# The convolution branch of an adaLN block: two nested running sums per tile in place of three products

## The chip, the core and the metric

The kernel runs on one core of a Trainium2 chip. The core has five engines with queues of their own: TensorE (PE, matrix products, with its weight loads shown apart as PEld), VectorE (DVE), ScalarE (ACT), GpSimd (POOL) and SyncE (SP, which here only issues DMAs). Each engine works through its own instructions strictly in the order in which they were written and waits on semaphores for the others. Products land in PSUM, where the kernel holds three accumulators `dn`, the bank `CV` of the convolution branch and four banks that `bank()` hands out in turn; everything else lies in SBUF or in device memory.

The metric is the device time of one execution in microseconds (us). Lower is better.

## The reference

`x` is 2048 tokens of 448 channels in float32. With `mod = silu(c) @ w_mod` cut into six rows `sa, ca, ga, sb, cb, gb`, the reference computes

```
h = layernorm(x) * (1 + ca) + sa
x = x + ga * A(h)                     # a state space model as a long convolution
h = layernorm(x) * (1 + cb) + sb
x = x + gb * ((silu(h @ w_gate) * (h @ w_up)) @ w_down)     # w_gate, w_up: 448x1792, w_down: 1792x448
```

where `A(h)[t, d] = sum over s <= t of K[d, t-s] * h[s, d], plus h[t, d] * Dskip[d]`, and `K[d, l]` is the real part of a sum over 256 complex exponentials in `l`.

## The kernel before, in words

**The small path.** When the exponents are small enough (a flag, computed on the chip, decides it, and with these inputs it does), the kernel takes `K[d, l]` as a straight line in `l`: `k0[d] + k1[d] * l`. The convolution is then made of running sums over tokens. Multiplied by `ga`, the two coefficients are kept as rows that are spread over all 128 partitions, `gm0` and `gm1` (which shares its tile with `g0`), and the gated skip row is `gd`. A running sum within a tile of 128 tokens is one product with a 128x128 triangle of ones, `tri`. What the tiles before add up to is carried as a row, `run0` and `run1`, which is added to the tile's first row ahead of the product; after the product the last row is copied out (to partition 127 of `run`, by way of the slice `end`, partitions 96 to 127) and a small DMA brings it to partition 0.

**Tiles and blocks.** The 2048 tokens are 16 tiles of 128. The feed-forward part treats them in six blocks of 2, 2, 3, 3, 3 and 3 tiles (`TILES`). In each block `f` runs over 14 slices of 128 hidden channels. For each `f`, `gate_up(f)` makes 22 products on PE (line 758), each as wide as the block (256 or 384 columns); ACT takes the silu (773), DVE multiplies (788), ACT rounds the result to `phi` (795) and DVE keeps the rest as `plo` (796); `down(f-1)` adds three products per tile into `dn` (808). The two halves of a split number, high and low, are each in fp32r, a form of float32. In the chain of work of the profile one fp32r product of 448 columns is a step of 0.20 us, one in plain float32 a step of 0.75 us. In the first block (`fresh`) the weights are still being loaded by DMAs on SP, and ACT and DVE split them into high and low parts on the way (lines 122 and 125 for `w_gate` and `w_up`, 115 and 117 for `w_down`).

**What sets the order.** The order is written out by hand (`manual_schedule`). While block `b` runs through the feed-forward part, the convolution branch of the next block's tiles is woven in: a table, `TIMES`, gives for each tile the half-steps at which its stages are recorded. Half-step `2f` stands right behind `gate_up(f)`, half-step `2f+1` right behind `down(f-1)`. The row of `TIMES` is the first for block 0, the second for block 1 and the third for all later blocks. All that a stage puts on PE, DVE, ACT, POOL or SP goes into that engine's queue at that place. In the first block and before it, two tiles are treated in a long opening part, whose order is the string `PLAN`.

**The stages before the change** are the functions of `small_path`. `s0` makes `h`, `s1` makes `v0 = h*gm0` and `v1 = h*gm1`, where `gm0` has meanwhile been lowered by the token's place in its tile times `gm1` (line 732, `ntok`). `s2` adds the carried rows (962, 963) and splits `v0` into `vh` and `vl` (970, 971). `s4` makes three products: `tri` with `vh` and `vl` into the bank `CV`, and `tri` with `v1` into one of the four banks that `gate_up` uses too (982 to 984). `s5` copies the carried rows out (1003 to 1005) and adds both sums to `x`, the second one times the token's place in its tile, `tok` (1006, 1007). For block 0's two tiles the first product is taken in plain float32 (`s4f`, 994 and 995).

`CV` is one PSUM bank. What is written there next has to wait until everything that reads the earlier contents is done.

Of the kernel before, what the change touches and what calls it, by code (L numbers as in the profile page):

```python
# [8 lines left out]
F32 = mybir.dt.float32  # L9
# [34 lines left out]
m1 cpc k1 gd h11 hd0 ck v01 sq0 o10 v10 w0 cbw o12 v11 o01 o02 hd1 w01 o13 o14 fs xh1 gc0 sa d00 gc1 st0 r0 sp x1 st1 r1 l1 spc n10 gq fl n11 D0 qtb sbt sbc  # L44
# [12 lines left out]
def tile_kernel(ctx, tc, x, a_re, a_im, b_re, b_im, c_re, c_im, log_dt,  # L57
# [71 lines left out]
    tok = const.tile([128, 1], F32)  # L129
# [8 lines left out]
    gm1 = g0  # L138
    ones = const.tile([128, 1], F32)
    halves = const.tile([128, 2], F32)  # L140
    mhalf, half = halves[:, 0:1], halves[:, 1:2]
    ntok = const.tile([128, 1], F32)
# [144 lines left out]
    with tc.tile_pool(name="pre", bufs=1) as pre:  # L287
# [20 lines left out]
        po.iota(tok, pattern=[[1, 1]], base=0, channel_multiplier=1, allow_small_or_imprecise_dtypes=True)  # L308
        po.iota(ntok, pattern=[[1, 1]], base=0, channel_multiplier=-1, allow_small_or_imprecise_dtypes=True)
# [25 lines left out]
        for z in range(2):  # L335
# [20 lines left out]
        h01, v0, v1, hd, h2 = ([pre.tile([128, w], t, name=f"{n}_{q}") for q in range(2)] for n, t, w in  # L356
                               (("h", F32, D), ("v0", F32, D), ("v1", F32R, D), ("hd", F32, D), ("h2", F32, 512)))
# [114 lines left out]
        def flag_of():  # L472
# [43 lines left out]
            "fr1": copy(run1[end], CV[end, 0:D]), "fx": copy(xs[0], DN[0][:, 0:D]),  # L516
# [204 lines left out]
    def first_rows():  # L721

        ve.tensor_tensor(run0[end], run1[end], DN[1][end, 0:D], op=OP.add)
# [6 lines left out]
    def gate_0():  # L730

        ve.scalar_tensor_tensor(gm0, gm1, ntok, gm0, op0=OP.mult, op1=OP.add)

    def run_blocks(pools, stages, first=None):
# [150 lines left out]
        for b, ts in enumerate(TILES):  # L885
            todo = {}
            if b + 1 < len(TILES):
# [16 lines left out]
                if b == 0 and first is None:  # L904
                    go(EXTRA[0], gate_0)
                    todo["mid"] = [(first_rows, ())]
                    at(0, 1, lambda: sy.dma_start(run[0:1], run[127:128]))
# [33 lines left out]
    def small_path(pools):  # L941
# [10 lines left out]
        def s1(i, on_v=False):  # L952
            h = vs[i]
            v0 = v0_of(i)
            v1 = work.tile([128, D], F32R, name="v1", bufs=2)
            for v, g in ((v0, gm0), (v1, gm1)):
                (ve if on_v else po).tensor_tensor(v, h, g, op=OP.mult)  # L957
            vs[i] = h, v0, v1

        def rows(i):  # L960
            h, v0, v1 = vs[i]
            ve.tensor_tensor(v0[0:1], v0[0:1], run0[0:1], op=OP.add)
            ve.tensor_tensor(v1[0:1], f32(v1[0:1]), run1[0:1], op=OP.add)

        def s2(i):
            rows(i)
            h, v0, v1 = vs[i]
            vh = work.tile([128, D], F32R, name="vh")
            vl = work.tile([128, D], F32R, name="vl")
            sc.copy(vh, v0)  # L970
            ve.tensor_tensor(vl, v0, f32(vh), op=OP.subtract)  # L971
            vs[i] = h, vh, vl, v1

        def s3(i, on_v=False):
            h = vs[i][0]
            (ve if on_v else po).tensor_tensor(h, h, gd, op=OP.mult)  # L976

        def s4(i):
            h, vh, vl, v1 = vs[i]
            o = CV[:, 0:D]  # L980
            s = bank()[:, 0:D]
            pe.matmul(o, tri, vh, start=True, stop=False)  # L982
            pe.matmul(s, tri, v1, start=True, stop=True)  # L983
# [133 lines left out]
```

## Time and profile before

| | |
|---|---|
| median of three runs | 471.46 us (470.68 to 472.36) |
| the profiled execution | 470.78 us, of which 469.0 us is the span from its first to its last instruction |
| granted TensorE clock, mean | 0.997 |
| PE busy | 459.0 us (98%) |
| DVE busy | 282.1 us (60%) |
| ACT busy | 160.5 us (34%) |
| POOL busy | 63.4 us (14%) |
| opening part, until the first product of `gate_up` | 31.75 us |
| block 0 (from 31.7 us) | 56.8 us |
| block 1 (from 88.5 us) | 55.5 us |
| blocks 2, 3 and 4 | 80.5 us each |
| block 5 with the tail | 83.5 us |

The span is the time from the first instruction to the last; 1.8 us of the execution lie outside it. The busy time of an engine is the time in which it had an instruction under way. Matmuls are pipelined, so the duration of one is longer than the step from one to the next: 12 products of 448 columns have a duration of 365 ns each, but the chain of work goes from one to the next in 200 ns. The view that follows the chain of work back from the last instruction gives these steps, and is the better price list for PE. Spans on POOL are rough.

### The profile page before, as it was taken

Reading aid. Unit: us, or ns where it says so; the run is one execution under the profiler, and the core shown is the slowest. Engines: PE = TensorE matmul, PEld = TensorE weight load, DVE = VectorE, ACT = ScalarE, POOL = GpSimd, SP = SyncE. Lnnn points to the kernel's source line nnn. Section 1 sums busy time; section 2 is a strip of 40 time slices with the busy share of each in tenths; the row PEclk is TensorE's granted clock in tenths of the full one; section 3 lists DMA queues with packets and bytes.
Section 4 is the critical chain, followed back from the end, with each engine's and each line's share of the span. In section 5 each row is a group of like instructions: output and inputs, shape, how many; then the busy total and the mean of one; then the engine's idle time right before and its main releaser. Section 6 shows DMA issues by size and latency. Waiting matters only on the chain.

```text
span 469.0 us, 7027 instructions
## 1 busy us (share of the span) xinstructions
PE 459.0 (98%) x2735; PEld 438.0 (93%) x2735; DVE 282.1 (60%) x539; ACT 160.5 (34%) x363; POOL 63.4 (14%) x88
## 2 busy tenths in 40 slices
PE   6899999999999999999999999999999999999995
PEld 4579999999999999999999999999999999999995
DVE  4888999778866447573754766374566543222225
ACT  5888666522343122233212223311223222221111
POOL 1232001000000223200022410003141000000000
PEclk9999999999999999999999999999999999999998
DMA  8976652110003000111300011130001112000001
GB/s 309 405 251 189 211 178 91 58 42 2 2 0 100 0 1 0 46 46 46 117 2 0 2 45 46 45 119 1 1 16 31 46 45 80 22 1 1 1 0 64
DMA packets 18778, 31.24 MB, mean 67 GB/s; under 512 B 2608, under 2 KB 13488, under 8 KB 18736
## 3 DMA queue, kind: packets, MB, share of 16 engines
q1 hardware_dynamic: 18096, 30.53, 19.3%
q8 instruction: 23, 0.38, 0.4%
q10 hardware_dynamic: 640, 0.18, 0.2%
q14 instruction: 19, 0.16, 0.1%
HBM read 24.61 MB, written 6.03 MB: 65 GB/s over the span
## 4 chain that ended last, share of the span: by engine, by line
PE 95%; issue 2%; DMA 1%; POOL 0%; ACT 0%; DVE 0%; POOLq 0%; ACTq 0%
PE bank L758 61%; PE dn L808 28%; DMA vec<-in_c_log_dt_dram 1%; PE dn L480 1%; PE bank L983 1%; PE cv L982 1%; PE bank L836 1%; PE cv L984 1%; PE bank L227 0%; PE bank L266 0%; PE bank L403 0%; PE cv L995 0%; PE bank L437 0%; ACT L339 0%; PE cv L375 0%
## 5 line engine op out<-in xcount | busy, mean ns | idle before, releaser
L758 PE MATMUL bank<-hhi,gu 128*128 128x384 f32 (+1 forms) x1176 | 208.9, 317 | 0.1
L758 PEld LDWEIGHTS bank<-hhi,gu 128*128 128x128 f32 x1176 | 189.4, 188 | 3.0 <-issue 0.8
L758 PE MATMUL bank<-hlo,gu 128*128 128x384 f32 (+1 forms) x672 | 130.8, 317 | 0.0
L758 PEld LDWEIGHTS bank<-hlo,gu 128*128 128x128 f32 x672 | 109.1, 188 | 0.2
L788 DVE TENSOR_TENSOR bank<-raw,bank 128x384 f32<-128x384 f32 (+1 forms) x69 | 36.9, 534 | 117.9 <-PE bank L758 115.4
L795 ACT CAST phi<-bank 128x384 fp32r<-128x384 f32 (+1 forms) x83 | 36.7, 443 | 137.9 <-DVE bank L788 137.9
L773 ACT ACTIVATE raw<-bank 128x384 f32<-128x384 f32 (+1 forms) x70 | 32.8, 469 | 119.4 <-PE bank L758 103.7
L796 DVE TENSOR_TENSOR plo<-bank,phi 128x384 fp32r<-128x384 f32 (+1 forms) x83 | 42.5, 512 | 37.5 <-ACT phi L795 37.5
L808 PE MATMUL dn<-wdh,phi 128*128 128x448 f32 x218 | 57.6, 365 | 0.0
L808 PE MATMUL dn<-wdh,plo 128*128 128x448 f32 x218 | 57.2, 363 | 0.0
L808 PE MATMUL dn<-wdl,phi 128*128 128x448 f32 x218 | 56.9, 362 | 0.0
L808 PEld LDWEIGHTS dn<-wdh,plo 128*128 128x128 f32 x218 | 40.8, 187 | 3.0 <-DVE plo L796 0.3
L808 PEld LDWEIGHTS dn<-wdl,phi 128*128 128x128 f32 x218 | 40.9, 187 | 2.7
L808 PEld LDWEIGHTS dn<-wdh,phi 128*128 128x128 f32 x218 | 38.7, 188 | 1.6 <-ACT p L773 0.2
L185 POOL TENSOR_SCALAR rsb<-mvb 128x1 f32<-128x1 f32 (+2 forms) x13 | 4.4, 337 | 142.6 <-DVE mvb L157 142.6
L125 DVE TENSOR_TENSOR gu<-raw,gu 128x1024 fp32r<-128x1024 f32 x14 | 17.0, 1218 | 0.9 <-ACT gu L123 0.9
L185 POOL TENSOR_SCALAR rsa<-mva 128x3 f32<-128x3 f32 (+1 forms) x6 | 2.3, 380 | 98.4 <-DVE mva L157 96.1
L957 POOL TENSOR_TENSOR m<-m,gm 128x448 f32<-128x448 f32 x9 | 10.4, 1155 | 20.8 <-DVE m L202 17.1
L971 DVE TENSOR_TENSOR vl<-m,vh 128x448 fp32r<-128x448 f32 x12 | 9.1, 757 | 6.7 <-ACT vh L970 6.1
L122 ACT CAST gu<-raw 128x768 fp32r<-128x768 f32 x14 | 11.6, 832 | 0.0
L976 POOL TENSOR_TENSOR m<-m,gd 128x448 f32<-128x448 f32 x9 | 11.5, 1281 | 0.0
L215 ACT ACTIVATE raw<-raw,rsb 128x64 f32<-128x64 f32 x14 | 4.8, 345 | 18.9 <-DVE raw L212 9.7
(237 smaller groups left out, 411.7 us busy)
## 6 DMA issues: line engine op xcount, KB each, us to landing
raw<-in_B_w_gate_up_dram SPq DMA_DIRECT2D x14, 512.0 KB, 3.8
rawd<-in_B_w_down_dram SPq DMA_DIRECT2D x16, 224.0 KB, 3.9
x<-in_A_u_dram SPq DMA_DIRECT2D x12, 224.0 KB, 2.8
out_dram<-x SPq DMA_DIRECT2D x11, 224.0 KB, 1.9
xd<-raw SPq DMA_DIRECT2D x9, 256.0 KB, 2.0
raw<-xd SPq DMA_DIRECT2D x36, 64.0 KB, 1.9
wm<-in_w_mod_groups_dram SPq DMA_DIRECT2D x5, 448.0 KB, 8.2
wm<-in_w_mod_groups_dram SPq DMA_DIRECT2D x5, 336.0 KB, 8.2
```

The lines of the kernel that those rows point to most:

```text
L122: sc.copy(wgu[j][:, :, 0:3, :], w[:, :, 0:3, :])
L125: ve.tensor_tensor(wgu[j][:, :, 3:7, :], w[:, :, ::-1, :], f32(wgu[j][:, :, 0:4, :][:, :, ::-1, :]), op=OP.subtract)
L185: po.tensor_scalar(rs[:, 0:n], self.mv[:, 0:n, 1], EPS, None, op0=OP.add)
L758: pe.matmul(ps[s][:, 0:n], w[:, s, a], (hlo if lo else hhi)[:, k, first_col(n):first_col(n) + n], start=first and q == 0, stop=end and q = ...
L773: sc.activation(p[:, 0:n], ps[0][:, 0:n], AF.Silu)
L788: ve.tensor_tensor(ps[1][:, 0:n], p[:, 0:n], ps[1][:, 0:n], op=OP.mult)
L795: sc.copy(hi[:, 0:n], ps[1][:, 0:n])
L796: ve.tensor_tensor(lo[:, 0:n], ps[1][:, 0:n], f32(hi[:, 0:n]), op=OP.subtract)
L808: pe.matmul(dn[q][:, 0:D], u[:, cs], v, start=f == 0 and z == 0, stop=f == (NF - 3 if last else NF - 1) and z == 2)
L957: (ve if on_v else po).tensor_tensor(v, h, g, op=OP.mult)
L971: ve.tensor_tensor(vl, v0, f32(vh), op=OP.subtract)
L976: (ve if on_v else po).tensor_tensor(h, h, gd, op=OP.mult)
```

## The change

The branch is computed by two running sums, one inside the other. The first, `u`, is the running sum of `h` itself. The second, `v`, is the running sum of `w = u*gm1`; since a running sum of a running sum weighs each token by how far back it lies, `u*(gm0-gm1) + v` is what was made before from `v0`, `v1` and the token's place. `gma` holds `gm0-gm1`.

From the second block on, `h` is rounded to `hh` for the first product, and what the rounding left off is multiplied by `gm0` and added into `w`, so that the second product carries it. In block 0 the first product takes `h` in plain float32 and there is no rest. Per tile there are thus two products, `u` (`s4` or `s4f`) and `v` (`s6`), and both are written to `CV`.

The stages become eight: `s0` (`h`), `s1` (`h*gd`, on POOL), `s2` (carried row, rounding, rest), `s3` (the rest times `gm0`, and the skip added to `x`, both on POOL), `s4` (`u`), `s5` (`w`, the first carried row out, `u*gma` added to `x` by POOL), `s6` (`v`), `s7` (the second carried row out, `v` added to `x`). In block 0, `row` and `skip` stand in the places of `s2` and `s3`. Each carried row has a DMA of its own (`carry`), for block 0's tiles on SP, for the others on ACT.

The opening part makes `hh` for its two tiles and sums these in `left_over`; `gate_0`, run early in block 0, turns the opening part's last rows into the new carried rows by three POOL instructions, and the DMA of that row moves from `f = 0` to `f = 2`. `tok`, `ntok` and their two iotas go.

The core of the diff (of the table `TIMES` only the row of block 0 is shown; `...` marks what is left out):

```diff
 TIMES = (
-    ((1, 3), 5, ((5, 10, 13, 15, 15, 16), (9, 9, 17, 19, 20, 20)), 20, (22, 23)),
+    ((1, 3), 5, ((5, 6, 7, 8, 10, 10, 14, 14, 16), (8, 9, 12, 13, 15, 15, 18, 18, 20)), 20, (22, 23)),
...
         def left_over():
             for q in range(2):
-                pe.matmul(CV[:, 0:D], all1, v1[q], start=q == 0, stop=q == 1)
+                pe.matmul(CV[:, 0:D], all1, hh[q], start=q == 0, stop=q == 1)
...
-            "fr1": copy(run1[end], CV[end, 0:D]), "fx": copy(xs[0], DN[0][:, 0:D]),
+            **{f"hh{q}": copy(hh[q], h01[q]) for q in range(2)}, "fr1": copy(run0[end], CV[end, 0:D]), "fx": copy(xs[0], DN[0][:, 0:D]),
...
     def first_rows():
-        ve.tensor_tensor(run0[end], run1[end], DN[1][end, 0:D], op=OP.add)
+        ve.tensor_copy(run1[end], DN[1][end, 0:D])
...
     def gate_0():
-        ve.scalar_tensor_tensor(gm0, gm1, ntok, gm0, op0=OP.mult, op1=OP.add)
+        t = v0_of(2)[end]
+        po.tensor_tensor(gma, gm0, gm1, op=OP.subtract)
+        po.tensor_tensor(t, run0[end], gma[end], op=OP.mult)
+        po.tensor_tensor(run1[end], run1[end], t, op=OP.subtract)
...
-                    at(0, 1, lambda: sy.dma_start(run[0:1], run[127:128]))
+                    at(2, 1, lambda: sy.dma_start(run[0:1], run[127:128]))
...
-        def s1(i, on_v=False):
+        def s1(i):
+            po.tensor_tensor(v0_of(i), vs[i], gd, op=OP.mult)
+
+        def row(i):
             h = vs[i]
-            v0 = v0_of(i)
-            v1 = work.tile([128, D], F32R, name="v1", bufs=2)
-            for v, g in ((v0, gm0), (v1, gm1)):
-                (ve if on_v else po).tensor_tensor(v, h, g, op=OP.mult)
-            vs[i] = h, v0, v1
...
+            ve.tensor_tensor(h[0:1], h[0:1], run0[0:1], op=OP.add)
 
         def s2(i):
-            rows(i)
-            h, v0, v1 = vs[i]
-            vh = work.tile([128, D], F32R, name="vh")
-            vl = work.tile([128, D], F32R, name="vl")
-            sc.copy(vh, v0)
-            ve.tensor_tensor(vl, v0, f32(vh), op=OP.subtract)
-            vs[i] = h, vh, vl, v1
+            row(i)
+            h = vs[i]
+            hh = work.tile([128, D], F32R, name="hh")
+            sc.copy(hh, h)
+            ve.tensor_tensor(h, h, f32(hh), op=OP.subtract)
+            vs[i] = h, hh
+
+        def skip(i):
+            po.tensor_tensor(xs[i], xs[i], v0_of(i), op=OP.add)
+
+        def s3(i):
+            h = vs[i][0]
+            po.tensor_tensor(h, h, gm0, op=OP.mult)
+            skip(i)
+
+        def s4f(i):
+            u = CV[:, 0:D]
+            pe.matmul(u, f32(tri), vs[i], start=True, stop=True)
+            vs[i] = None, u
 
         def s4(i):
-            h, vh, vl, v1 = vs[i]
-            o = CV[:, 0:D]
-            s = bank()[:, 0:D]
-            pe.matmul(o, tri, vh, start=True, stop=False)
-            pe.matmul(s, tri, v1, start=True, stop=True)
-            pe.matmul(o, tri, vl, start=False, stop=True)
-            ve.tensor_tensor(xs[i], h, xs[i], op=OP.add)
-            vs[i] = o, s
...
+            h, hh = vs[i]
+            u = CV[:, 0:D]
+            pe.matmul(u, tri, hh, start=True, stop=True)
+            vs[i] = h, u
+
+        def carry(i, k, row):
+            if i + 1 < NT:
+                sc.copy(run[end, k, :], row[end])
+                (sy if i in TILES[1] else sc).dma_start(run[0:1, k, :], run[127:128, k, :])
 
         def s5(i):
-            o, s = vs.pop(i)
-            if i + 1 < NT:
-                sc.copy(run1[end], s[end])
-                ve.scalar_tensor_tensor(run0[end], run1[end], 128.0, o[end], op0=OP.mult, op1=OP.add)
-                (sy if i in TILES[1] else sc).dma_start(run[0:1], run[127:128])
-            ve.tensor_tensor(xs[i], xs[i], o, op=OP.add)
-            ve.scalar_tensor_tensor(xs[i], s, tok, xs[i], op0=OP.mult, op1=OP.add)
+            h, u = vs[i]
+            t = work.tile([128, D], F32, name="t")
+            w = work.tile([128, D], F32R, name="w")
+            ve.tensor_tensor(t if h is not None else w, u, gm1, op=OP.mult)
+            if h is not None:
+                ve.tensor_tensor(w, t, h, op=OP.add)
+            ve.tensor_tensor(w[0:1], f32(w[0:1]), run1[0:1], op=OP.add)
+            carry(i, 0, u)
+            ve.tensor_tensor(t, u, gma, op=OP.mult)
+            po.tensor_tensor(xs[i], xs[i], t, op=OP.add)
+            vs[i] = w
+
+        def s6(i):
+            v = CV[:, 0:D]
+            pe.matmul(v, tri, vs[i], start=True, stop=True)
+            vs[i] = v
+
+        def s7(i):
+            v = vs.pop(i)
+            carry(i, 1, v)
+            ve.tensor_tensor(xs[i], xs[i], v, op=OP.add)
+
+        return lambda b: (s0, s1, s2, s3, s4, s5, s6, s7) if b else (s0, s1, row, skip, s4f, s5, s6, s7)
```

How this moves instructions is seen best in block 0, around `f = 7`. In the rows below, `tri` is the triangle, `m` with a number is the tile that holds `h`, `w` the weighted first sum, `dn` the accumulators of `down`, `gu` the weights of `gate_up`, `wdl` the low part of a slice of `w_down`, and `x_74` and `x_75` are block 0's two branch tiles, the first and the second. On PE, before, the two products of the first tile stand behind `down(6)`, the plain float32 one last:

```order
L808 MATMUL dn_68<-wdh_664,plo 128x448
L808 MATMUL dn_69<-wdh_664,plo 128x448
L994 MATMUL bank<-v_766,tri 128x448
L995 MATMUL cv<-m_79,tri 128x448
L758 MATMUL bank<-hhi,gu_662 128x256 x7
```

On PE, now, the first tile's second sum (1007) stands ahead of `down(6)` and the second tile's first sum (978) behind it:

```order
L1007 MATMUL cv<-w,tri 128x448
L809 MATMUL dn_68<-wdh_667,phi 128x448
L809 MATMUL dn_69<-wdh_667,phi 128x448
L809 MATMUL dn_68<-wdl_668,phi 128x448
L809 MATMUL dn_69<-wdl_668,phi 128x448
L809 MATMUL dn_68<-wdh_667,plo 128x448
L809 MATMUL dn_69<-wdh_667,plo 128x448
L978 MATMUL cv<-m_79,tri 128x448
L759 MATMUL bank<-hhi,gu_665 128x256 x7
```

Two products that both write `cv` now have one `down`, six products, between them, and the second of them is of another tile. On DVE, before, at the same `f`:

```order
L788 TENSOR_TENSOR bank<-p,bank 128x256
L125 TENSOR_TENSOR gu_709<-raw,gu_709 128x2x512
L796 TENSOR_TENSOR plo<-bank,phi 128x256
L976 TENSOR_TENSOR m_79<-m_79,gd 128x448
L997 TENSOR_TENSOR x_74<-m_79,x_74 128x448
L1004 SCALAR_TENSOR_TENSOR run<-run,cv 32x448
L1006 TENSOR_TENSOR x_74<-x_74,cv 128x448
L1007 SCALAR_TENSOR_TENSOR x_74<-bank,tok,x_74 128x448
L117 TENSOR_TENSOR wdl_764<-rawd_83,wdh_763 128x448
```

And on DVE, now:

```order
L789 TENSOR_TENSOR bank<-p,bank 128x256
L126 TENSOR_TENSOR gu_714<-raw,gu_714 128x2x512
L797 TENSOR_TENSOR plo<-bank,phi 128x256
L1013 TENSOR_TENSOR x_74<-x_74,cv 128x448
L996 TENSOR_TENSOR w<-cv,g_89 128x448
L999 TENSOR_TENSOR w<-w,run 1x448
L1001 TENSOR_TENSOR t<-cv,gma 128x448
L118 TENSOR_TENSOR wdl_768<-rawd_83,wdh_767 128x448
```

The reader of the first tile's second sum (1013) stands behind the feed-forward's multiply, the split of a weight slice and `plo`; behind it come the readers of the second tile's first sum (996, 1001), with the carried row between them (999). On POOL, block 0 had only small instructions of the norms from the branch on:

```order
L1048 COMPARE_AND_BRANCH
L177 TENSOR_SCALAR cs<-mva 128x1
L178 TENSOR_SCALAR mva<-mva 128x1
L177 TENSOR_SCALAR cs<-mva 128x1
L178 TENSOR_SCALAR mva<-mva 128x1
L185 TENSOR_SCALAR rsa<-mva 128x2
L186 TENSOR_TENSOR rsa<-rsa,halves 128x2
L177 TENSOR_SCALAR cs<-mvb 128x1
```

Now the three instructions of `gate_0` stand ahead of the norms' small ones (they are lines 731, 732 and 733, of which the first, `gma<-gm_90,g_89`, has 128 partitions and the other two have 32), and the branch's work follows the norms:

```order
L185 TENSOR_SCALAR rsa<-mva 128x2
L186 TENSOR_TENSOR rsa<-rsa,halves 128x2
L954 TENSOR_TENSOR m_79<-m_79,gd 128x448
L969 TENSOR_TENSOR x_74<-x_74,m_79 128x448
L954 TENSOR_TENSOR m_79<-m_79,gd 128x448
L1002 TENSOR_TENSOR x_74<-x_74,t 128x448
L969 TENSOR_TENSOR x_75<-x_75,m_79 128x448
L1002 TENSOR_TENSOR x_75<-x_75,t 128x448
L177 TENSOR_SCALAR cs<-mvb 128x1
```

Nine instructions of 448 columns, the three of `gate_0` among them, have come to POOL in this block: for each tile the skip row (954), its addition to `x` (969) and the addition of the first sum's share (1002).

More of the change, by code (lines that the diff above doesn't have):

```diff
@@ L138, in tile_kernel @@
     gm1 = g0
+    gma = const.tile([128, D], F32)
     ones = const.tile([128, 1], F32)
@@ L141, in tile_kernel @@
     mhalf, half = halves[:, 0:1], halves[:, 1:2]
-    ntok = const.tile([128, 1], F32)
     pick = const.tile([128, 1], F32)
@@ L355, in tile_kernel @@
         sca = pre.tile([128, N], F32)
-        h01, v0, v1, hd, h2 = ([pre.tile([128, w], t, name=f"{n}_{q}") for q in range(2)] for n, t, w in
-                               (("h", F32, D), ("v0", F32, D), ("v1", F32R, D), ("hd", F32, D), ("h2", F32, 512)))
+        h01, v0, v1, hd, hh, h2 = ([pre.tile([128, w], t, name=f"{n}_{q}") for q in range(2)] for n, t, w in
+                               (("h", F32, D), ("v0", F32, D), ("v1", F32R, D), ("hd", F32, D), ("hh", F32R, D), ("h2", F32, 512)))
         qt = {n: pre.tile([128, 512], F32, name="qt" + n) for n in "gcs"}
```

26 lines of the change are left out of this document (4 added, 22 removed), and 2 rows, old and new, of the table TIMES.

## The prediction

> **What bounds the kernel now.** I read the engines' busy times first, then the shares of the chain of work, then the busy times by stage, and last the chain itself.
>
> ```profile
> PE 459.0 (98%) x2735; PEld 438.0 (93%) x2735; DVE 282.1 (60%) x539; ACT 160.5 (34%) x363; POOL 63.4 (14%) x88
> PE 95%; issue 2%; DMA 1%; POOL 0%; ACT 0%; DVE 0%; POOLq 0%; ACTq 0%
> core 0: us, PE busy (x) PEld busy (x) DVE busy (x) ACT busy (x) POOL busy (x), PEclk, DMA share, GB/s
> 31.70:88.50 56.80, 56.75 (x410) 54.11 (x411) 52.55 (x97) 40.77 (x95) 5.44 (x10) 1.00 0.48 147
> 144.00:224.50 80.50, 80.50 (x445) 78.75 (x444) 45.12 (x82) 21.53 (x44) 14.74 (x17) 1.00 0.11 35
> ```
>
> PE is the bound: 95% of the chain. But the stages differ. Over the whole span DVE is busy for 60%, in block 2 (144.0 to 224.5) for 56%, in block 0 (31.7 to 88.5) for 52.55 of 56.80, which is 93%. A product saved is a gain in either, as long as PE is not made to wait for DVE, and in block 0 DVE has 4.25 us to spare in all.
>
> **What each tile loses on PE.** The chain in block 2, around one tile's products, by start and step:
>
> ```profile
> 170.30 3.81 PE bank L758 x22
> 174.12 0.20 PE cv L982
> 174.32 0.21 PE bank L983
> 174.53 0.20 PE cv L984
> 174.73 1.80 PE dn L808 x9
> ```
>
> Three products take 0.61, so one is 0.203. The twelve tiles 4 to 15 each lose one (two remain, each of the same width): 12 x 0.203 = 2.44 us gained. The products now stand alone between `gate_up` and `down`, not three in a row; each of the rows above has the same 0.20 whether a product follows another form or its own, so I take 0.20 for a lone one. Block 0's two tiles are the ones made here for block 1:
>
> ```profile
> 58.10 2.51 PE bank L758 x22
> 60.61 1.20 PE dn L808 x6
> 61.81 0.20 PE bank L994
> 62.02 0.75 PE cv L995 x2
> 62.77 2.60 PE bank L758 x22
> ```
>
> They have 0.20 and 0.75 before, and still do: the plain product is now that of `h`, the other that of `w`. No gain here.
>
> **The bank `CV` in block 0.** Here the change adds a wait. Before, one of a tile's two products in block 0 was written there, and two `f` lay between the tiles (the chain above has the first tile's at 62.02). Now the first tile's second sum (1007) is written to `CV` behind `gate_up(7)`, and the second tile's first sum (978) behind `down(6)`, six products later. It must wait until DVE has read the former (1013), and behind that wait stands all of PE's work.
>
> When does PE get there? `gate_up(7)` ends at 60.61 in the row above; the first tile's plain product now stands ahead of it, so 61.36; the second sum 0.20, `down(6)` 1.20: 62.76.
>
> When is DVE done with 1013? DVE goes strictly in order, and in this stretch it is the row of instructions itself that counts:
>
> ```profile
> 47.18 0.42 DVE L788 TENSOR_TENSOR bank<-p,bank 128x256 f32<-128x256 f32 x1
> 48.98 0.61 DVE L117 TENSOR_TENSOR wdl<-rawd,wdh 128x448 fp32r<-128x448 f32 x1
> 49.60 0.43 DVE L788 TENSOR_TENSOR bank<-p,bank 128x256 f32<-128x256 f32 x1
> 51.41 0.68 DVE L200 SCALAR_TENSOR_TENSOR m<-x,mva,ca 128x448 f32<-128x448 f32 x1
> 52.84 0.62 DVE L957 TENSOR_TENSOR m<-m,gm 128x448 f32<-128x448 f32 x1
> 53.38 0.62 DVE L957 TENSOR_TENSOR v<-m,g 128x448 fp32r<-128x448 f32 x1
> 59.66 0.60 DVE L962 TENSOR_TENSOR m<-m,run 1x448 f32<-1x448 f32 x1
> 61.26 0.41 DVE L788 TENSOR_TENSOR bank<-p,bank 128x256 f32<-128x256 f32 x1
> 63.06 0.60 DVE L976 TENSOR_TENSOR m<-m,gd 128x448 f32<-128x448 f32 x1
> ```
>
> From one multiply (788) to the next, with nothing of the branch between, are 2.42 us (47.18 to 49.60). `h` for a tile (200, 202) adds 1.43 (51.41 to 52.84), a product by a row 0.54 (52.84 to 53.38), and one partition costs as much as 128 (0.60 beside 0.62). From a multiply to what follows `plo` are 1.80 (61.26 to 63.06). Now between the multiplies of `f = 4` and `f = 7` stand three such rounds, `h` of the second tile, the three of the first tile's `s5` (996, 999, 1001) and one carried row; one more carried row has come ahead of `f = 4`. A read of a bank is taken at 0.62, the duration of 985 further below, so `s5` is 0.62 + 0.54 + 0.62 = 1.8. The products by rows (957) that stood here are gone. 49.60 + 0.54 + 3 x 2.42 + 1.43 + 1.8 + 0.54 = 61.17 for the multiply of `f = 7`. With the 1.80 and 0.62 for 1013 itself that is 63.59. It can't be earlier than its bank: `gate_up(7)` now ends at 61.36, and a multiply follows 0.12 behind (174.23 below against 174.11), so 61.48 + 1.80 + 0.62 = 63.90 at best. PE, there at 62.76, waits at least 63.90 - 62.76 = 1.14. If DVE is late by C us for other causes, it waits 0.83 + C (from 63.59; valid from C = 0.31 on).
>
> **The carried row in block 0.** Its DMA moves from `f = 0` to `f = 2`, on SP, past two pairs of weight loads:
>
> ```profile
> 39.35 0.63 SPq L907 DMA_DIRECT2D run<-run  x1
> DMA to landing us min/median/max: 4.8/4.8/4.8
> 45.04 0.33 SPq L105 DMA_DIRECT2D raw<-in_B_w_gate_up_dram  x1
> 45.41 0.42 SPq L110 DMA_DIRECT2D rawd<-in_B_w_down_dram  x1
> ```
>
> Before it was issued at 39.35 and landed 4.8 later. Now it is issued behind the load of 45.41, at 45.83, again right behind one load of each weight; at the same 4.8 it lands at 50.63. DVE wants the row (958) behind `plo` of `f = 3`, where 48.98 stands above. It waits 1.65, between 0 (a landing within 3.1) and 1.65, and I take 1.65 since that is the one landing that this stage shows.
>
> **POOL beside DVE.** POOL gets five instructions of 448 columns up to this place: 954, 969, 954, 1002, 969. In block 0 POOL had none so wide, so the nearest rows are from later:
>
> ```profile
> 185.65 1.16 POOL L957 TENSOR_TENSOR v<-m,g 128x448 fp32r<-128x448 f32 x1
> 186.13 1.16 DVE L971 TENSOR_TENSOR vl<-m,vh 128x448 fp32r<-128x448 f32 x1 [1.48 <-ACT vh L970]
> 201.79 0.63 DVE L971 TENSOR_TENSOR vl<-m,vh 128x448 fp32r<-128x448 f32 x1 [0.57 <-ACT vh L970]
> L957 POOL TENSOR_TENSOR m<-m,gm 128x448 f32<-128x448 f32 x9 | 10.4, 1155 | 20.8 <-DVE m L202 17.1
> ```
>
> The same DVE instruction takes 0.63 alone and 1.16 when it starts 0.48 into one of POOL's: 0.53 lost. In block 0 DVE has such instructions nearly without pause (126, 118, 958, each with two operands in SBUF; 797 and 789 have one in PSUM), so each of POOL's should meet one. The first of the five falls ahead of the row's wait and is covered by it; four remain. The price of one lies between 0, if DVE is never the one held up (no gain, since no row shows a DVE instruction that a running POOL one makes shorter), and 0.53 + 0.48 = 1.01, if DVE starts together with POOL's. I take 0.53, the row itself: 4 x 0.53 = 2.12. [...]
>
> So C = 1.65 + 2.12 = 3.77, and the wait of PE in block 0 is 0.83 + 3.77 = 4.60 us.
>
> **The rest, at nothing.** `gate_0`, three on POOL early in block 0, can hold up DVE's splits of weights, each by at most 1.01; on the other side a 0.68 goes from DVE:
>
> ```profile
> 38.27 0.68 DVE L732 SCALAR_TENSOR_TENSOR gm<-g,ntok,gm 128x448 f32<-128x448 f32 x1
> 42.37 0.62 DVE L117 TENSOR_TENSOR wdl<-rawd,wdh 128x448 fp32r<-128x448 f32 x1 [1.08 <-ACT wdh L115]
> ```
>
> DVE idles for 1.08 at 42.37, which takes that up; without that cover it is 0 to +0.5. The two copies of `hh` in the opening part fall into ACT's idle time:
>
> ```profile
> 26.25 0.56 ACT L481 COPY g<-dn 128x448 f32<-128x448 f32 x1
> 27.86 0.53 ACT L395 COPY qts<-bank 128x448 f32<-128x448 f32 x1 [1.06 <-PE bank L269]
> ```
>
> Two copies at 0.56 against 1.06 of idle time: nothing, at most 0.1. The first tile's second carried row goes out on SP while PE is held up, and lands (62.2 + 4.8 = 67.0) before 999 of the second tile is reached, at about 68; without the hold-up it costs 0 to 1.0. In blocks 1 to 4 a tile's next product comes 3.81 + 1.80 + 0.20 = 5.81 us after the last:
>
> ```profile
> 174.23 0.56 DVE L788 TENSOR_TENSOR bank<-raw,bank 128x384 f32<-128x384 f32 x1 [2.17 <-PE bank L758]
> 175.81 0.62 DVE L985 TENSOR_TENSOR x<-m,x 128x448 f32<-128x448 f32 x1
> ```
>
> In between DVE has a multiply and a `plo` (0.56 each) and the branch's four (996, 997, 999, 1001; 0.62 each): 3.6, with two meetings with POOL 4.7. That fits; DVE had idled 2.17 here. The stages' other moves are within that.
>
> **The sum.** -2.44 + 4.60 = +2.16. The profiled execution is 470.78, so 472.9 by its own time. It lies 0.68 under the median of the runs, 471.46; by the median 473.6.
>
> **Rivals.** *POOL's instructions cost DVE their whole length.* For: DVE has hardly a pause in block 0. Four at 1.01 are 4.04, C 5.69, the wait 6.52, the change +4.08: 475.5.
>
> *POOL is the one that waits.* DVE is nearly always at work, so POOL may come second each time, and the row's wait is all: C 1.65, the wait 2.48, change +0.04: 471.5. Against it is the row at 186.13, where DVE came second; for it that DVE idled ahead of that one.
>
> *The row is there in time too.* The landing is then under 3.1 us after an earlier issue; the wait for `CV` stays with its 1.14, change -1.30: 470.2.
>
> *The whole gain comes (faster).* It decides at 62.76: if DVE is through with 1013 by then, nothing waits, and the time is 470.78 - 2.44, by the median 469.0. For that the 1.14 would have to go from between the bank and 1013, nearly the whole of the split of weights there (126; with the multiply and `plo` it makes the 1.80): as when its steps between 61.26 and 63.06 were long only for the sake of what else ran there. Against it: the 1.80 is measured in a stretch where DVE waited for nothing.
>
> *Blocks 1 to 4 wait too.* If POOL's norms come late behind its own new work and with them the next `h`, a product misses its 5.81 by a collision, 0.5 in each of four blocks: 473.6 + 2.0 = 475.6. Against: 1.1 of room by the sum above. Here also belongs that a lone product costs more than 0.20, so that the change does not save what it says.
>
> **How the numbers follow.** Forecast 0.31, whole length 0.17, POOL waits 0.18, row in time 0.16, whole gain 0.08, later blocks 0.10. A measurement of this kernel tells about 0.3%, which is 1.4 us: faster is under 470.05, slower over 472.87. Faster: 0.08, and half of the 0.16, whose 470.2 lies at the bound: 0.16. Same: the other half, the 0.18 and 0.02 of the forecast's lower end: 0.28. Slower: 0.29 + 0.17 + 0.10 = 0.56. The range reaches from the whole gain, 468.9, to beyond the two dear cases, 476.3, with 0.7 of the carried row's 1.0 on top of them; outside are some 0.05 below and 0.1 above. The forecast's own range is 472.5 to 474.8 (the landing 1.1 earlier; collisions at 0.83).
>
> **What the profile after would show.** In block 0 the chain has, instead of an unbroken row of PE, a piece of DVE's 1013 (with 126 and 797 ahead of it) before PE's 978, and a gap of some 4.6 us there; block 0 lasts 61 us in place of 56.8. DVE idles 1.65 ahead of the first 958, released by a DMA. Instructions 126, 118 and 958 with a POOL one beside them are longer by 0.5. Blocks 2 to 4 take 79.9 (three products of 0.20 less) in place of 80.5, and block 1's 55.5 becomes 54.9. If the gap at 978 is under 1.1, or if block 0 is long for waits elsewhere, the working is wrong; if later blocks aren't shorter by 0.2 for each tile, the gain is.

## The result and the profile after

The changed kernel takes 474.66 us in the median of five runs (474.04 to 476.14), the kernel before 471.46. The ratio is 1.0073 with a 95% interval from 1.0049 to 1.0098: slower by 0.7%. The profiled execution is the one of 474.66, with a span of 472.5 us (before: 470.78 and 469.0).

The page of the changed kernel (two lines of it), and the same two stages as before (busy times by stage):

```profile
PE 459.2 (97%) x2723; PEld 436.7 (92%) x2723; DVE 279.5 (59%) x522; ACT 169.8 (36%) x378; POOL 101.1 (21%) x116
PE 87%; DVE 5%; ACT 3%; issue 3%; DMA 1%; POOL 0%; DVEq 0%; POOLq 0%; ACTq 0%
31.60:94.20 62.60, 58.95 (x409) 54.92 (x410) 52.15 (x89) 41.71 (x97) 18.15 (x18) 0.97 0.42 133
149.50:229.40 79.90, 79.90 (x442) 78.17 (x441) 44.68 (x81) 23.68 (x47) 17.88 (x20) 1.00 0.11 35
```

PE has twelve products fewer, and its share of the chain has gone from 95% to 87%. Block 0, in these windows, takes 62.6 where it took 56.8, and PE isn't busy all the time there any more. Block 2 takes 79.9 where it took 80.5. Taken from the starts of the blocks' first products, which is more exact, the stages compare so (us; block 5 starts at 385.31 in the kernel before):

| stage | before | after | difference |
|---|---|---|---|
| opening part | 31.75 | 31.65 | -0.10 |
| block 0 | 56.58 | 62.45 | +5.87 |
| block 1 | 55.52 | 55.26 | -0.26 |
| blocks 2, 3, 4 | 241.46 | 239.62 | -1.84 |
| block 5 and tail | 83.7 | 83.6 | -0.1 |
| span | 469.0 | 472.5 | +3.5 |

The whole loss lies in block 0, and most of it at one place. The chain of work there, in the changed kernel:

```profile
61.44 1.09 DVE gu L126
...
62.92 1.24 DVE m L958
64.15 0.53 DVE wdl L118
64.69 0.34 DVE bank L789
65.03 1.01 DVE gu L126
66.08 0.41 DVE plo L797
66.49 0.54 DVE x L1013
67.07 1.64 PE cv L978 x2
68.71 3.52 PE bank L759 x22
72.23 1.20 PE dn L809 x6
```

And PE's own row of that product in the timeline, with the idle time ahead of it and who ended it:

```profile
67.07 1.64 PE L978 MATMUL cv<-m,tri 128*128 128x448 f32 x2 [3.34 <-DVE x L1013]
```

DVE comes late to 1013, the read of the first tile's second sum, and PE waits 3.34 for it. Then something follows that was in no part of the prediction: the plain product takes 1.64 in place of 0.75, and `gate_up` behind it 3.52 in place of 2.51; from 72.23 on the pace is the old one. Together that is 0.89 + 1.01 = 1.90. The busy times of these stretches show why (the last three columns are the granted TensorE clock, the DMA share and GB/s; the last row lies from one change of the clock to the next):

```profile
62.80:67.07 4.27, 0.81 (x3) 0.30 (x3) 4.22 (x7) 1.65 (x4) 0.88 (x1) 1.00 0.57 177
67.07:68.70 1.63, 1.63 (x3) 0.82 (x4) 0.00 (x0) 0.00 (x0) 0.00 (x0) 0.58 0.86 221
68.70:72.20 3.50, 3.50 (x24) 3.50 (x23) 2.21 (x4) 2.21 (x5) 0.29 (x1) 0.71 0.30 113
72.20:75.90 3.70, 3.70 (x30) 3.62 (x29) 2.62 (x5) 2.71 (x8) 2.00 (x3) 1.00 0.10 29
67.34:70.74 3.40, 3.40 (x13) 2.60 (x13) 0.74 (x2) 1.09 (x2) 0.00 (x0) 0.50 0.67 213
```

The 0.58 and 0.71 are means over stretches that mix two clocks. The granted clock is 0.50 from 67.33 to 70.74, which is 3.41 us, and 1.00 before and behind that. PE is busy all that time, so by estimate half of it, 1.7, is lost; the other 0.2 of the 1.90 is close to what the first product behind a gap cost at a clock of 1.00 in the kernels with a known delay further below, 0.47 in place of 0.20. 3.34 + 1.90 = 5.24 of the 5.87. The other 0.6 lies at `gate_up(2)`, where the split (126) that meets `gate_0`'s last instruction on POOL is late, with 2.00 in place of 1.22, and at two products with `plo`, 0.3 late.

Why DVE is late shows in its timeline:

```profile
48.23 1.85 DVE L126 TENSOR_TENSOR gu<-raw,gu 128x1024 fp32r<-128x1024 f32 x1
50.33 1.23 DVE L958 TENSOR_TENSOR m<-m,run 1x448 f32<-1x448 f32 x1
52.36 1.21 DVE L126 TENSOR_TENSOR gu<-raw,gu 128x1024 fp32r<-128x1024 f32 x1
56.00 1.85 DVE L126 TENSOR_TENSOR gu<-raw,gu 128x1024 fp32r<-128x1024 f32 x1
61.44 1.22 DVE L126 TENSOR_TENSOR gu<-raw,gu 128x1024 fp32r<-128x1024 f32 x1 [0.58 <-ACT gu L124]
62.92 1.24 DVE L958 TENSOR_TENSOR m<-m,run 1x448 f32<-1x448 f32 x1
```

beside POOL's:

```profile
47.52 1.47 POOL L954 TENSOR_TENSOR m<-m,gd 128x448 f32<-128x448 f32 x1 [0.89 <-DVE m L202]
49.07 2.02 POOL L969 TENSOR_TENSOR x<-x,m 128x448 f32<-128x448 f32 x1
55.36 1.41 POOL L954 TENSOR_TENSOR m<-m,gd 128x448 f32<-128x448 f32 x1 [4.27 <-DVE m L202]
61.50 2.17 POOL L969 TENSOR_TENSOR x<-x,m 128x448 f32<-128x448 f32 x1
```

Four of DVE's instructions overlap with one of POOL's and are longer by 0.63 each (1.85 against 1.22, 1.24 against 0.61): 2.5 us. In these rows the one that started later was the longer one: POOL's 969 starts at 49.07 and at 61.50 while DVE's 126 is under way and takes 2.02 and 2.17, where POOL's shortest rows of this size take 1.15; 126 at 61.44 keeps its 1.22, but the 958 that DVE starts behind it, at 62.92, falls into POOL's lengthened instruction. The 0.58 ahead of 61.44 is another wait: ACT was late with the high part of the weights.

### The profile page after: what moved, and what is told of

Same layout as the page of the kernel before. It is cut to its first block, busy times and chain, and to the rows that moved or that the text cites. A ratio compares the mean times of both kernels' runs of the same rounds, so it can differ in the third digit from the quotient of the medians.

```text
span 472.5 us, 7094 instructions
## 1 busy us (share of the span) xinstructions
PE 459.2 (97%) x2723; PEld 436.7 (92%) x2723; DVE 279.5 (59%) x522; ACT 169.8 (36%) x378; POOL 101.1 (21%) x116
## 4 chain that ended last, share of the span: by engine, by line
PE 87%; DVE 5%; ACT 3%; issue 3%; DMA 1%; POOL 0%; DVEq 0%; POOLq 0%; ACTq 0%
PE bank L759 56%; PE dn L809 25%; DVE gu L126 2%; DMA vec<-in_c_log_dt_dram 1%; PE dn L478 1%; DVE wdl L118 1%; PE cv L1007 1%; ACT gu L123 1%; PE cv L984 1%; PE bank L837 1%; DVE plo L797 0%; DVE bank L789 0%; PE bank L266 0%; ACT gu L124 0%; PE cv L978 0%
## 5 line engine op out<-in xcount | busy, mean ns | idle before, releaser
L973 POOL TENSOR_TENSOR m<-m,gm 128x448 f32<-128x448 f32 x12 | 13.9, 1160 | 61.0 <-DVE m L965 61.0
L954 POOL TENSOR_TENSOR m<-m,gd 128x448 f32<-128x448 f32 x14 | 17.5, 1252 | 19.7 <-DVE m L202 19.7
L1002 POOL TENSOR_TENSOR x<-x,t 128x448 f32<-128x448 f32 x10 | 12.8, 1276 | 36.3 <-DVE t L1001 36.3
L126 DVE TENSOR_TENSOR gu<-raw,gu 128x1024 fp32r<-128x1024 f32 x14 | 19.6, 1400 | 1.5 <-ACT gu L124 1.5
L989 ACT COPY run<-cv 32x448 f32<-32x448 f32 x26 | 13.7, 527 | 12.7 <-DVE t L996 6.5
L969 POOL TENSOR_TENSOR x<-x,m 128x448 f32<-128x448 f32 x10 | 13.4, 1342 | 0.1
L202 DVE SCALAR_TENSOR_TENSOR m<-m,rsa,sa 128x448 f32<-128x448 f32 x14 | 12.7, 908 | 1.2 <-DVE m L200 0.5
```

What stands on the lines that cost most here:

```text
L126: ve.tensor_tensor(wgu[j][:, :, 3:7, :], w[:, :, ::-1, :], f32(wgu[j][:, :, 0:4, :][:, :, ::-1, :]), op=OP.subtract)
L954: po.tensor_tensor(v0_of(i), vs[i], gd, op=OP.mult)
L969: po.tensor_tensor(xs[i], xs[i], v0_of(i), op=OP.add)
L973: po.tensor_tensor(h, h, gm0, op=OP.mult)
L989: sc.copy(run[end, k, :], row[end])
L1002: po.tensor_tensor(xs[i], xs[i], t, op=OP.add)
```

## Experiments

In all of them the opening part varies between 31.6 and 33.6 us from one execution to another, so stages are compared from block 0's first product on.

### The wait in `CV` taken away

One row of `TIMES`, the second tile of block 0:

```diff
-(8, 9, 12, 13, 15, 15, 18, 18, 20)), 20, (22, 23)),
+(8, 9, 14, 15, 17, 17, 20, 20, 20)), 20, (22, 23)),
```

> The changed kernel with one line of the table altered: in block 0 the second tile's first sum is recorded at half-step 17 in place of 15, its second at 20 in place of 18, its carried row at 14. Theory (PE waits in CV for 1013, DVE being late, and the idle time lowers the granted clock): no idle time of PE ahead of 978, the granted clock stays at 1.00, block 0 is about 5.2 us shorter, the time is 469.0 to 470.0. Rival (DVE's lateness itself is the bound in block 0, CV only the place where it shows): PE waits as long at another place of block 0, in a product with plo or in the second sum, and the time stays above 473.

Measured: 469.87 against 471.14 before, ratio 0.9975 (0.9955 to 0.9994). PE doesn't wait at 978, the clock stays at 1.00 in every stretch of block 0, and block 0 takes 57.30, 5.15 less than in the changed kernel. So the order of two products that share a bank, with one `down` between them, made nearly the whole loss. Not all of DVE's lateness is gone: block 0 is 0.7 longer than in the kernel before, 0.4 of it at `gate_up(2)` and 0.3 at the products with `plo` a step earlier. PE's timeline there:

```profile
63.41 0.56 PE L809 MATMUL dn<-wdl,phi 128*128 128x448 f32 x2
64.08 0.67 PE L809 MATMUL dn<-wdh,plo 128*128 128x448 f32 x2
```

Two products at 0.20 from 63.41 on end their steps at 63.81, so the next is 0.27 late. Two of the expectations further below speak of a wait of 0.9 here. That is the length of DVE's piece in the chain of work (63.18 to 64.08), during which PE was making the products shown; it is no idle time of PE.

### POOL's part in it

Without POOL's six instructions on block 0's tiles:

```diff
-            po.tensor_tensor(v0_of(i), vs[i], gd, op=OP.mult)
+            if i not in TILES[1]:
+                po.tensor_tensor(v0_of(i), vs[i], gd, op=OP.mult)
```

and so for 969 and 1002.

> The changed kernel without POOL's five instructions on block 0's tiles up to the wait (954, 969, 1002; six in all): h*gd and u*gma are not added to x for these two tiles, so this part of the computation is left out. Theory (POOL's instructions lengthen DVE's): 126 and 958 return to 1.22 and 0.60, PE idles ahead of 978 for 0.5 to 1.5 in place of 3.34, the clock is not lowered, 470 to 471. Rival (order of DVE's own work and the bank alone make the wait): it stays near 3.3, and the time within 0.5 of 474.7.

Measured: 472.90, ratio 1.0026 (1.0009 to 1.0042). The rows that were longer are at their length again, but in the profiled execution the wait is 2.18, more than was expected, and the clock goes down as far as before. PE's timeline:

```profile
65.62 1.60 PE L980 MATMUL cv<-m,tri 128*128 128x448 f32 x2 [2.18 <-DVE x L1016]
```

DVE's timeline in the same run:

```profile
48.47 1.22 DVE L126 TENSOR_TENSOR gu<-raw,gu 128x1024 fp32r<-128x1024 f32 x1
50.58 0.61 DVE L959 TENSOR_TENSOR m<-m,run 1x448 f32<-1x448 f32 x1 [0.56 <-DMA run<-run]
```

And the busy times just behind the gap, with the granted clock third from the end:

```profile
67.00:69.00 2.00, 2.00 (x11) 1.98 (x10) 0.63 (x1) 1.01 (x2) 0.00 (x0) 0.50 0.63 247
```

Taking 2.5 us of prolongation away brought 1.70 in block 0 (62.45 to 60.75) and only 1.16 of the wait. Below it lay the wait for the carried row's DMA (0.56), which DVE had been too late to feel, and the same 0.57 for ACT's weights. So the collisions are about a third of the wait; DVE's own row of work in that stretch, with what it waits for, is the rest. Behind what is left, 2.18, the clock was 0.50 in the profiled execution. Over the ten executions of this run the mean granted clock is 0.993 to 0.996 in six, which took 472.78 to 474.17, and 0.998 to 1.000 in four, which took 471.17 to 472.49. Only one of them was traced, so that the gap makes this difference is likely but not shown.

With the six on DVE instead:

```diff
-            po.tensor_tensor(v0_of(i), vs[i], gd, op=OP.mult)
+            (ve if i in TILES[1] else po).tensor_tensor(v0_of(i), vs[i], gd, op=OP.mult)
```

> The changed kernel with the same six instructions of block 0 on DVE in place of POOL. DVE has 5 x 0.54 = 2.7 more of its own ahead of the wait and loses the prolongations, some 4.4 in all by the trace (three of 126 or 118 by 0.63, two of 958 by 0.63, and their overlaps). Theory: the wait ahead of 978 is 1.5 to 2.5 and the time 471.5 to 473.5. Rival (POOL takes work off DVE at no price): the wait is 3.3 + 2.7 = 6, the time 477 or more.

Measured: 475.39, ratio 1.0080 (1.0050 to 1.0110); block 0 takes 62.43, the wait is 3.38:

```profile
68.13 1.02 PE L978 MATMUL cv<-m,tri 128*128 128x448 f32 x2 [3.38 <-DVE x L1013]
```

Both numbers in the expectation were wrong, and the result lies between them: the same block and the same wait as with POOL (62.45, 3.34). Five instructions at 0.54 are 2.7; the prolongations are four at 0.63, 2.5, and not the 4.4 that the expectation counted. Here the six instructions cost block 0 as much on POOL as on DVE itself.

### What a gap in PE costs

The kernel before, with a known delay ahead of the first tile's two products in block 0, on DVE:

```diff
             ve.tensor_tensor(v0[0:1], v0[0:1], run0[0:1], op=OP.add)
+            for _ in range(9 if i == TILES[1][0] else 0):
+                ve.tensor_tensor(v0[0:1], v0[0:1], run0[0:1], op=OP.add)
```

> The kernel before, with nine more additions of the first carried row on one partition put ahead of the first tile's two products of block 0 on DVE (the row is then added ten times, which changes the result of that tile and of those behind it). They hold PE up there: 9 x 0.54 = 4.9 less the 1.1 of room that the trace shows between 963 and 994, so 3.8 of idle time. Theory (idle time of PE above some length lowers the clock that is granted for a few us afterwards): the time grows by more than the idle time, 3.8 + 1.7 = 5.5, to 477.0, with a granted clock under 0.8 behind the gap. Rival (the low clock of the changed kernel comes from something else, as the plain float32 product alone behind the gap): 475.3, clock 1.00.

> The kernel before with three such additions in place of nine. By the step of 0.625 and the room of 0.77 seen with nine (9 x 0.625 - 4.85), PE idles 3 x 0.625 - 0.77 = 1.1. Theory (the clock goes down only behind an idle time above some length, which lies between the 0.9 that left it at 1.00 in e1 and the 2.18 that lowered it in e2): two outcomes tell where; if 1.1 is under it, block 0 grows by 1.1 and the clock stays at 1.00, else by about 3.0. Rival (the cost behind the gap is in proportion to the gap): 1.1 x 1.9 / 3.34 = 0.6 on top, 1.7 in all.

> The same with four additions: PE idles 4 x 0.625 - 0.77 = 1.7. Theory of a length: block 0 grows by 1.7 with the clock at 1.00, or by 1.7 + 1.9 = 3.6 with a low clock. Rival of proportion: 1.7 + 1.0 = 2.7.

With nine additions, the row of PE's timeline with the gap, and then the busy times from one change of the clock to the next (the granted clock is the third number from the end):

```profile
66.50 0.74 PE L996 MATMUL bank<-v,tri 128*128 128x448 f32 x1 [4.85 <-DVE v L965]
```

```profile
64.42:71.24 6.82, 4.74 (x16) 3.88 (x17) 6.65 (x12) 1.53 (x4) 0.00 (x0) 0.50 0.22 72
```

The same two views with four additions, the second just behind the gap:

```profile
64.36 0.47 PE L996 MATMUL bank<-v,tri 128*128 128x448 f32 x1 [1.72 <-DVE v L965]
```

```profile
64.30:68.10 3.80, 3.74 (x26) 3.35 (x27) 3.73 (x8) 2.63 (x6) 0.00 (x0) 1.00 0.13 32
```

And with three:

```profile
62.92 0.47 PE L996 MATMUL bank<-v,tri 128*128 128x448 f32 x1 [1.07 <-DVE v L965]
```

```profile
63.00:65.00 2.00, 2.00 (x12) 1.61 (x13) 2.00 (x4) 1.17 (x3) 0.00 (x0) 1.00 0.06 24
```

| additions | gap | block 0 against before (56.58) | lowest clock around the gap | time |
|---|---|---|---|---|
| 3 | 1.07 | +1.56 | 1.00 | 472.47 (one execution) |
| 4 | 1.72 | +2.21 | 1.00 | 474.26 (one execution) |
| 9 | 4.85 | +7.14 | 0.50 | 479.14, ratio 1.0172 (1.0137 to 1.0207) |

A gap of 1.07 or 1.72 costs itself, and 0.5 for the start of the product behind it (0.47 in place of 0.20) and for a second short wait of 0.30 at the next tile. The 2.21 lies between the 1.7 and the 2.7 that were expected, and the clock decides: a price in proportion to the gap would have given 0.6 and 1.0 on top with a lower clock, and it was 0.5 both times at 1.00. The gap of 4.85 costs 2.3 on top. Its clock is at 0.50 already from 64.41 on, in the middle of the gap, and until 71.24; PE is busy for 4.74 of that, and half of 4.74 is 2.4. So the gaps of 1.07 and 1.72 left the clock at 1.00, around the one of 4.85 it was 0.50, and the plain float32 product is not the cause: in this kernel a product in fp32r stands first behind the gap. The one execution with four additions has an opening part 0.9 longer than the kernel before, which is why its time is up by more than its block. By the medians nine additions cost 8.0, more than the 6.8 between the profiled spans; I leave the difference open.

### ACT's copy ahead of DVE's reads

e1 with the carried row's copy recorded first in `s5` for block 0's tiles. In the changed kernel ACT's copy stands in its queue until DVE has read the bank:

```profile
58.75 0.53 ACT L989 COPY run<-cv 32x448 f32<-32x448 f32 x1 [2.25 <-DVE w L996]
```

```diff
+            if h is None:
+                carry(i, 0, u)
             ve.tensor_tensor(t if h is not None else w, u, gm1, op=OP.mult)
...
-            carry(i, 0, u)
+            if h is not None:
+                carry(i, 0, u)
```

> e1 with one more edit: in block 0 the copy of the first sum's last row (ACT, 989) is recorded ahead of DVE's two reads of the bank in place of between them. The traces of the changed kernel and of e1 show it in ACT's queue until DVE has read (2.25 idle ahead of 989), ahead of the split of the next weights, for whose rest (126) DVE then idles 0.57. Theory: that 0.57 goes, PE's wait of 0.9 for plo of f = 6 in e1 shrinks to 0.4 or less, and the time is 0.3 to 0.6 under that of e1, 469.3 to 469.6. Rival (DVE is late by its collisions alone): the 0.57 turns up elsewhere, time as e1.

Measured: 469.86, ratio 0.9972 (0.9958 to 0.9986). In block 0 it did what was expected: DVE no longer idles ahead of 126, the products with `plo` are in time, PE has no wait left that the timeline marks, and the block takes 56.81 (busy times by stage):

```profile
31.90:88.70 56.80, 56.66 (x409) 53.73 (x410) 51.58 (x88) 42.04 (x97) 22.34 (x18) 1.00 0.49 147
```

But the time is that of e1: in the profiled executions block 1 has grown from 55.45 to 55.90 and given it back. The chain of work leads to block 1's first sum from the load of the next `x`, which is issued only after block 0's last store.

```profile
91.18 0.34 SPq L872
...
91.63 4.31 DMA rawd<-in_A_u_dram
...
105.30 0.49 PE cv L984
```

That this load made block 1 longer is not shown. In e1 it is issued just as far into the block, 2.96 us, and took 4.06 in place of 4.31, so it can account for 0.25 of the 0.45 at most.

### Block 1

Four tables for block 1 follow, the first on top of e1, the other three on top of e6. Earlier:

```diff
-((4, 4, 6, 6, 8, 8, 11, 11, 14), (5, 7, 11, 11, 13, 13, 16, 16, 17), (14, 15, 16, 16, 18, 18, 21, 21, 21)),
+((4, 4, 5, 5, 7, 7, 11, 11, 14), (5, 7, 11, 11, 13, 13, 16, 16, 17), (14, 15, 16, 16, 18, 18, 21, 21, 21)),
```

> e1 with block 1's first tile earlier in the table: s2 and s3 at half-step 5, s4 and s5 at 7, in place of 6 and 8. In the changed kernel PE waits in block 1 by 0.35 in all around that tile (block 1 takes 55.26 where 55.52 - 0.61 = 54.91 was left). Theory (w of that tile is late for its second sum): block 1 takes 54.9 to 55.1, and the time is 0.4 under that of e1. Rival (the carried row of block 0 isn't there by half-step 5): PE waits at the first sum, time equal to or above that of e1.

Measured: 470.66, ratio 0.9993 (0.9981 to 1.0004); block 1 takes 56.10. Earlier was the wrong way: PE waits 0.40 at the first sum. The chain reaches that sum from the load by way of POOL's 954, for which DVE idles 1.26 ahead of the carried row.

Later, in three ways, each against the row that was removed above:

```diff
+((4, 4, 7, 7, 9, 9, 12, 12, 14), (5, 7, 12, 12, 14, 14, 17, 17, 18), (14, 15, 17, 17, 18, 18, 21, 21, 21)),
```

> e6 with block 1's stages later, not earlier: the first tile's s2 and s3 at 7, its sums at 9 and 12; the second tile's at 14 and 17, the third's at 18 and 21 (before: 8 and 11, 13 and 16, 18 and 21). The traces of e6 and e5 show the first tile's chain in block 1 begin with the load of x at the end of block 0, which lands some 7.3 us into the block, and reach the first sum at 105.30, half a us late. Theory (block 1's first tile is bound by that load, so what is drawn together there waits): block 1 takes 54.9 to 55.2 in place of 55.90, and the time is 0.7 to 1.0 under that of e6, 468.9 to 469.2. Rival (the collisions of DVE with POOL in block 1 make the wait wherever it stands): 55.5 or more, time as e6.

```diff
+((4, 4, 6, 6, 8, 8, 12, 12, 14), (5, 7, 12, 12, 14, 14, 17, 17, 18), (14, 15, 17, 17, 18, 18, 21, 21, 21)),
```

> As e8, but the first tile's first sum stays at 8 (s2 and s3 at 6) and only its second goes to 12, so that DVE has longer for w. Theory of the load: the first sum waits as in e6 (0.3 to 0.5), w has time: block 1 takes 55.1 to 55.4, the time lies between e6 and e8. If the time between the two sums is what counts, it equals e8.

```diff
+((4, 4, 7, 7, 9, 9, 12, 12, 14), (5, 7, 12, 12, 14, 14, 17, 17, 18), (14, 15, 16, 16, 19, 19, 22, 22, 22)),
```

> As e8, but the second tile's second sum (17) and the third tile's first (now 19) stand two half-steps apart, the third's carried row at 16, its second sum at 22. In e8 the first tile's sums waited for nothing (106.97, 113.38) and block 1 lost 2.03 us of idle time at the third tile's first sum alone, whose carried row stood on DVE behind the read of the bank before it. Theory: no idle time of PE over 0.5 in block 1, the clock stays at 1.00, block 1 takes 54.9 to 55.3, the time is 468.8 to 469.3. Rival (the last tile's later stages delay the start of block 2): a wait of 0.5 or more at block 1's end, time at 470 or above.

Measured: e8 471.88, ratio 1.0018 (1.0000 to 1.0036), block 1 57.05; e9 472.16, ratio 1.0014 (0.9999 to 1.0029), block 1 58.73; e10 471.78, ratio 1.0013 (0.9993 to 1.0033), block 1 57.82. The theory failed in all three; in e10 what its rival named came, a wait of 0.82 near the block's end and a time above 470. In e8 the first tile's two sums wait for nothing (106.97 and 113.38 in the chain), as expected. But the table has made a new wait at the third tile: in e8 and e9 the carried row stands on DVE behind the read of the bank before, in e10 the third tile's first sum itself waits for that read, 1.38. Each of the four tables moved the wait, and none removed it; a table that leaves all three tiles of block 1 free was not found. The fastest versions are therefore e1 and e6, both under the kernel before.

e8 and e9 showed one thing by chance. Both have the same gap, to 0.01. In e8, PE's timeline and the busy times behind it:

```profile
127.14 0.48 PE L984 MATMUL cv<-hh,tri 128*128 128x448 f32 x1 [2.03 <-ACT hh L964]
```

```profile
127.20:129.50 2.30, 2.30 (x15) 2.20 (x16) 1.84 (x4) 0.67 (x2) 1.67 (x2) 1.00 0.02 7
```

And in e9, the second row from one change of the clock to the next:

```profile
128.50 0.48 PE L984 MATMUL cv<-hh,tri 128*128 128x448 f32 x1 [2.04 <-ACT hh L964]
```

```profile
129.70:133.10 3.40, 3.40 (x17) 3.32 (x16) 3.04 (x7) 0.90 (x3) 1.74 (x2) 0.50 0.03 5
```

Behind 2.03 the clock stays at 1.00; behind 2.04, in e9's execution, it is 0.50 for 3.41 us, and e9's block 1 is longer than e8's by 1.68, 1.54 of it behind the gap.

## Why the prediction was right, point by point

The time lies in the range, the direction is the forecast's, and 474.66 is 1.1 above the 473.6, within the forecast's own 472.5 to 474.8. The mechanism was the one named: PE waits at 978 for DVE's 1013, and e1, which takes that wait alone away, turns the loss into a gain. But that the sizes agree is in part luck: two errors cancel.

**The gain** was 12 x 0.203 = 2.44. Blocks 2 to 4 have 79.87, where 79.9 was said, and lose 0.61 each. Block 1 loses 0.26 only. What the prediction set at nothing there ("that fits") costs 0.35: DVE's two additions for the first tile meet POOL and take 1.01 and 0.79, the product behind waits, and a product behind a wait takes 0.47 (chain of work):

```profile
112.88 1.01 DVE w L998
113.88 0.02 issue
113.91 0.79 DVE w L999
...
115.95 0.47 PE cv L1007
```

**The wait at 978** was 4.60 and is 3.34. Four steps of that sum, one by one. The carried row's wait of 1.65 was wrong: it is 0 in the changed kernel and 0.56 where POOL's six are left out (e2). Its DMA was issued at 46.61 and not 45.83 and landed 3.6 later, at 50.2; DVE itself came to 958 only at 50.33, where 48.98 was assumed. The collisions, 4 x 0.53 = 2.12, are four at 0.63, 2.5, but not the four that were meant: the first 954, which the row's wait was to cover, cost its 0.63, and 1002 cost nothing. The wait for ACT (0.58) was missed: the sum has nothing for the copy in ACT's queue, which stands there until DVE has read. And PE came there at about 63.7, not 62.76, since it had lost 0.4 at `gate_up(2)` and 0.3 at the products with `plo`; there the prediction had set `gate_0` at nothing, covered by DVE's 1.08 of idle time at 42.37. That cover comes later than the product at 39.30 which waits. In all, 1013 was done at 67.03, where the forecast has 63.59 + 3.77 = 67.36: close, though its terms were not. Of these errors, -1.65, +0.4 and +0.58 leave 0.3 that is not traced to an instruction. A small misreading in the working made no difference: the 0.62 for a read of a bank is taken from 985, which reads no bank; 1013 took 0.54 in the chain.

**The clock** is the error on the other side. The prediction took a wait of PE at its own length. In this kernel it cost 1.90 more, 1.7 of it from 3.41 us at half the clock. Without it the sum of 3.34 and the small waits less the gain would have been +1.6; with it, +3.5.

**The rivals.** The whole length of a POOL instruction was not paid (0.63 against 1.01 at most); that POOL waits in its turn was half right, as 969 took 2.02 and 2.17 where POOL's shorter rows of this size take 1.16, but DVE paid too. That the row is there in time came true, and did not decide. Of the later blocks only block 1 waits, for the 0.35; blocks 2 to 4 do not. The whole gain needed 1013 to be done in time; e6 shows a time of 469.86 where the forecast for that case was 469.0.

**What the profile after was to show:** a piece of DVE in the chain ahead of 978 (seen, with 126 and 797 ahead), a gap of 4.6 (3.34), block 0 of 61 (62.45), DVE idle for a DMA ahead of 958 (not seen), prolongations of 0.5 (0.63), blocks 2 to 4 at 79.9 (seen), block 1 at 54.9 (55.26).

## What to carry to other kernels

When products are moved, ask for each accumulation bank what reads its old contents, and count what that engine has ahead of the read; one table row, with the same work and the same products, made 1% here. In a stage where DVE had been busy for 93% and POOL's instructions lengthened its own by 0.63 each, work given to POOL was not given away: block 0 took 62.45 with it there and 62.43 with it on DVE. And the bound engine's waits are not always priced at their own length alone: the 3.34 here cost 1.90 more. Look at the clock, from one of its changes to the next, and at the first products behind each gap.

## What the runs showed of the hardware that had not been expected

In the profiled executions the granted clock stayed at 1.00 behind idle times of PE of 1.07 (three additions), 1.38 (e10), 1.72 (four additions) and 2.03 us (e8). Behind 2.04 (e9), 2.18 (e2), 3.34 (the changed kernel) and 3.38 (e3) it went down to 0.50 for 3.4 us, and around 4.85 (nine additions) for 6.8. By the chain of work the gaps of 2.18, 3.34 and 3.38 cost 1.9 beside their own length, of which 1.7, half of 3.4, is the clock by estimate, and the one of 4.85 cost 2.3. What decides between e8's 2.03 and e9's 2.04 is not shown: each of these kernels was traced in one execution.

The other: of a DVE and a POOL instruction that overlap in block 0 of the changed kernel, both with two operands in SBUF, the one that started later was the longer one, and where each came into the other's way in turn both lost: 0.63 a piece on DVE's side (1.85 in place of 1.22 and 1.24 in place of 0.61), and up to 2.17 in place of 1.15 on POOL's. DVE's 797 at 50.00 and 789 at 55.67, each with one operand in PSUM, kept 0.41 and 0.42 beside POOL's 969 and 954. e3 gives the balance for this stage: with the work on DVE, block 0 took 62.43, with POOL 62.45.
